# An attention and mixture-of-experts kernel on one core: the vector engines' work of the last part ranked by the step that needs it, and the last two units' steps mixed

## The chip, the cores and the metric

The kernel runs on one core of a Trainium2 chip. The metric is the device time of one execution, in microseconds. The engines go by these names: PE is TensorE's matmuls and PEld its weight loads, DVE is VectorE, ACT is ScalarE, POOL is GpSimd, SP is SyncE, which only issues transfers. Each has its own queue and works through it in the order in which the program was written.

## The reference, cut to what matters

```python
x = attention(q, k, v)                 # 2304 tokens x 512, masks local / strided by head
p = probs / probs.sum(-1)              # 2304 x 4 experts
out = 0
for e in range(4):
    h = relu(x @ w1[e])                # 512 -> 1024
    out += p[:, e:e+1] * (h @ w2[e])   # 1024 -> 512
```

All values are f32, and so is the result.

## The kernel before, in words

The eight pairs of an expert and a half of its hidden channels (512 of 1024) are called units. The tokens are handled in three parts: 384 in a first part that runs beside the attention, 896 in a second (`plan_unit`), and 1024 in the last part (`plan_second`), the only one that the change touches. The last part takes some 300 us of the span.

**The products.** Both layers of a unit are 2x2 block products in Winograd's form of Strassen's scheme: seven products instead of eight. Each product is one step. There are seven h steps for the first layer (P1, s1, s2, s3, s4, P2, a22, named after the block of weights) and seven o steps for the second. A step has two halves f, and each half is six matmuls of 128x128 weights on 512 columns (line 897), since each f32 value is split into a high and a low fp32r part and three of the four partial products are taken. A step is therefore 12 matmuls.

**PSUM.** Steps of kind a (P1, s2, s3, a22) add onto one pair of buffers one after the other; kind b (P2) and kind c (s1, then s4) do so in theirs. The running sum has to be read by another engine after every step, before the next step of the kind adds to it. h steps of kind a use the tag ps (two buffers), o steps of kind a the tag sc (two buffers); kinds b and c use mo (four buffers), except that o P2 uses ps.

**The other engines' work.** After h P2, h s1 and h s4 the product is copied by ACT (line 919, tile v, the code's `park`). After h P1, s2 and s3 DVE adds a parked copy to the product (line 928, `finish`), giving the tile q, and then takes relu and multiplies by the expert's probability, which is laid out along the columns in the tile pb (line 931); after h a22 line 931 alone does this, straight from PSUM. `plan_t` makes the second layer's seven operands T (b11, t1, t2, b22, t3, b21, t4) from q: differences of q blocks (line 960), a high part (ACT, line 955) and a low part (line 956). Lines 956 and 960 can go to DVE or POOL (engine class VP). After each o step DVE adds the product to the tile acc (line 1005). Seven weight blocks per layer and unit are loaded again from DRAM by SP: first layer by `reload` (line 1033), second layer into a ring of four buffers (`plan_ring`, line 983). After the last unit the eight acc tiles are stored (line 1008).

**The order.** PE's order is written out: `TURN` lists 14 steps of a unit, and in it stand the first two h steps of the next unit ("next P2", "next s1") between the h steps of this one:

```python
TURN = ("h P1", "h s4", "h s2", "next P2", "h s3", "next s1", "h a22", "o P1", "o s1", "o s2", "o s4", "o s3", "o P2", "o a22")
```

The last unit has no next unit, so both of those fall away there. The order of the other engines is found by a planner (`Plan.walk`) when the program is built: each operation has a modelled duration and a rank (the last numbers of `add`, written `z`, `zz`), and an engine takes, of the operations that can start earliest, the one of the lowest rank. An operation of class VP goes to the engine that would end it sooner by the model. The planner never lets an engine wait for an operation of better rank. `dz` is the modelled time of half a step (1.365 us). The result is a fixed list for each engine; the chip runs it in that order, with semaphores where an operation needs another's result or buffer.

Before, the rank of an operation was the time of the step that makes its input, with a few half steps added.

Of the kernel before, what the change touches and what calls it, by code (L numbers as in the profile page):

```python
# [11 lines left out]
AF = mybir.ActivationFunctionType  # L12
# [294 lines left out]
def attn_moe_kernel(  # L307
# [13 lines left out]
    nc = tc.nc  # L321
# [587 lines left out]
    def plan_h(u, step, z, dz):  # L909
# [12 lines left out]
        def finish(r, c, nm, f, key, zz):  # L922
            tok = f"q{r}{c}{f}"
            q = lambda: late["q"][r, c, f]
            src = lambda: held[key][:, 0:TH2]
            if nm:
                i = late[nm, f]
                add("DVE", DD, lambda: nc.vector.tensor_tensor(out=q(), in0=src(), in1=late["u"][i], op=ALU.add),  # L928
                    [key, f"u{i}", "late3"], [tok], zz)
            from_q = bool(nm)  # L930
            add("DVE", DD, lambda: nc.vector.scalar_tensor_tensor(  # L931
                out=q(), in0=q() if from_q else src(), scalar=0.0, in1=late["p"][:, c * TH2:c * TH2 + TH2], op0=ALU.max, op1=ALU.mult),
                ["pb", "late3"] + ([] if nm else [key]), [tok], zz + 0.1, two=from_q)

        for f in range(2):
# [5 lines left out]
            if step in PARK:  # L941
                park(f, key, ze)
            else:
                r, c, nm = DONE[step]
                finish(r, c, nm, f, key, ze)

    def plan_t(step, z, dz):
# [4 lines left out]
        def put(v, nm, j, zz):  # L952
            src, tok = v
            hi, lo = (lambda: late["T"][nm][0][j]), (lambda: late["T"][nm][1][j])
            add("ACT", TH2 / 1200 + 0.17, lambda: nc.scalar.activation(out=hi(), in_=src(), func=AF.Copy), [tok, "late3"], [f"T{nm}h{j}"], zz)  # L955
            add("VP", VP, lambda e: engine(e).tensor_tensor(out=lo(), in0=src(), in1=hi().bitcast(F32), op=ALU.subtract),
                [tok, f"T{nm}h{j}"], [f"T{nm}l{j}"], zz)

        def sub(dst, a, b, zz):
            add("VP", VP, lambda e: engine(e).tensor_tensor(out=dst[0](), in0=a[0](), in1=b[0](), op=ALU.subtract), [a[1], b[1]], [dst[1]], zz)  # L960

        for j in range(2):
            if step == "P1":
                put(q[0, 0, j], "b11", j, z)
            elif step == "s2":
                sub(q[0, 0, j], q[0, 1, j], q[0, 0, j], z)
                put(q[0, 0, j], "t1", j, z)
            elif step == "s3":
                sub(q[0, 0, j], q[1, 1, j], q[0, 0, j], z)
                put(q[0, 0, j], "t2", j, z)  # L970
                put(q[1, 1, j], "b22", j, z + 2 * dz)
                sub(q[0, 1, j], q[1, 1, j], q[0, 1, j], z + 4 * dz)
                put(q[0, 1, j], "t3", j, z + 4 * dz)
            else:
                put(q[1, 0, j], "b21", j, z + 2 * dz)
                sub(q[1, 0, j], q[1, 0, j], q[0, 0, j], z + 4 * dz)
                put(q[1, 0, j], "t4", j, z + 4 * dz)
# [9 lines left out]
    acc_count = {}  # L987

    def plan_o(u, step, slot, first, last, z, dz):
# [32 lines left out]
    def plan_second():  # L1022
# [4 lines left out]
        for step in ("P2", "s1"):  # L1027
            plan_h(seq[0], step, zz, dz)
            zz += 2 * dz
# [6 lines left out]
        if NU > 1:  # L1036
            reload("P2", seq[1], zz)
            reload("s1", seq[1], zz)
        for i, u in enumerate(seq):
            v = seq[i + 1] if i + 1 < NU else None  # L1040
            w = seq[i + 2] if i + 2 < NU else None
            slots = {}
            fetch = list(FETCH)
            for _ in range(RING):
                st = fetch.pop(0)
                slots[st] = plan_ring(u, st, zz)
            for what in TURN:
                kind, step = what.split()
                if kind == "next":
                    if v is None:  # L1050
                        continue
                    plan_h(v, step, zz, dz)
                    if w is not None:
                        reload(step, w, zz + 6 * dz)
                elif kind == "h":
                    plan_h(u, step, zz, dz)
                    if step in ("P1", "s2", "s3", "a22"):
                        plan_t(step, zz + 2 * dz, dz)
                    if v is not None:
                        reload(step, v, zz + 6 * dz)  # L1060
                    if step == "a22" and v is not None and units[v][0] != units[u][0]:
                        plan_p(v, zz + 4 * dz)
                else:
                    plan_o(u, step, slots[step], i == 0, i == NU - 1, zz, dz)
                    if fetch:
                        st = fetch.pop(0)
                        slots[st] = plan_ring(u, st, zz)
                zz += 2 * dz
# [225 lines left out]
```

## Time and profile before

| | before |
|---|---|
| device time, median of 3 runs | 824.32 us (823.99 to 825.2) |
| profiled execution, device time | 825.78 us |
| profiled execution, span | 824.0 us |
| PE busy | 810.3 us (98%) |
| DVE busy | 625.2 us (76%) |
| ACT busy | 330.6 us (40%) |
| POOL busy | 308.3 us (37%) |

The span runs from the first to the last instruction; the profiled execution's device time is 1.78 us more. "Busy" is the share of the span in which the engine worked, an average over all parts. PE's busy time counts matmuls, whose ends are modelled.

### The profile page before, as it was taken

How to read it: one execution, taken by the hardware profiler on the slowest of the kernel's cores; microseconds unless marked ns; L12 is line 12 of the kernel's file. 1: busy time of each engine (PE TensorE's matmuls, PEld its weight loads, DVE VectorE, ACT ScalarE, POOL GpSimd, SP SyncE). 2: the span in 40 equal slices, each digit the busy share in tenths (PEclk: the TensorE clock that was granted, in tenths of full speed). 3: DMA queues.
4: the chain of work that ended last, by engine and by line, in shares of the span. 5: the costliest groups of instructions: out<-in, count | busy, mean ns of one | idle time of the engine just before them, and what ended most of it. 6: DMA issues, size and time to landing. Idle time of an engine off the chain costs nothing.

```text
span 824.0 us, 13898 instructions
## 1 busy us (share of the span) xinstructions
PE 810.3 (98%) x5385; PEld 686.0 (83%) x5388; DVE 625.2 (76%) x892; ACT 330.6 (40%) x616; POOL 308.3 (37%) x243
## 2 busy tenths in 40 slices
PE   8999999999999999999999999999999999999987
PEld 6888888999889888888989888887878787878765
DVE  6877867865588776868677693959796979788886
ACT  4643556444336353543535352524142323323140
POOL 5431332934173542515344270305050505142352
PEclk9999999999999999999999999999999999999998
DMA  9685532339578686867753405747474556635714
GB/s 336 218 312 183 204 138 83 102 125 330 211 256 283 258 307 236 324 212 293 260 205 128 175 30 180 278 157 249 148 251 172 188 211 173 232 125 204 208 48 153
DMA packets 70401, 168.69 MB, mean 205 GB/s; under 512 B 5152, under 2 KB 22720, under 8 KB 70336
## 3 DMA queue, kind: packets, MB, share of 16 engines
q1 hardware_dynamic: 70192, 167.73, 57.5%
q8 instruction: 42, 0.69, 0.3%
q14 instruction: 23, 0.19, 0.1%
q10 hardware_dynamic: 144, 0.08, 0.1%
HBM read 108.00 MB, written 59.79 MB: 204 GB/s over the span
## 4 chain that ended last, share of the span: by engine, by line
PE 95%; DVE 1%; DMA 1%; issue 1%; POOL 1%; ACT 0%; POOLq 0%; ACTq 0%
PE mo L897 21%; PE mo L750 17%; PE ps L897 16%; PE sc L897 15%; PE mo L734 8%; PE ps L750 5%; PE sc L750 5%; PE ps L561 2%; PE sc L479 1%; PE ps L533 1%; PE sc L474 1%; DMA qkL<-in_qk_local 1%; PE ps L569 1%; POOL q L960 1%; PE mo L1205 1%
## 5 line engine op out<-in xcount | busy, mean ns | idle before, releaser
L960 POOL TENSOR_TENSOR q<-q,q 128x512 f32<-128x512 f32 x31 | 44.8, 1445 | 211.9 <-DVE q L931 186.2
L750 PE MATMUL mo<-w2t,h 128*128 128x512 f32 x336 | 80.8, 389 | 0.0
L750 PEld LDWEIGHTS mo<-w2t,h 128*128 128x128 f32 x336 | 63.1, 188 | 13.0
L750 PE MATMUL mo<-w2t,hs 128*128 128x512 f32 x288 | 69.9, 395 | 0.0
L750 PEld LDWEIGHTS mo<-w2t,hs 128*128 128x128 f32 x288 | 53.0, 188 | 11.0
L741 DVE SCALAR_TENSOR_TENSOR h<-c,h 128x448 fp32r<-128x448 f32 x48 | 59.6, 1268 | 2.4 <-ACT h L738 1.0
L645 POOL TENSOR_TENSOR a<-raw,a 128x512 fp32r<-128x512 f32 x22 | 34.1, 1549 | 59.6 <-DVE c L1097 44.9
L644 ACT ACTIVATE w2t<-raw 128x512 fp32r<-128x512 f32 x60 | 36.8, 629 | 37.8 <-PE mo L750 24.7
L1005 DVE TENSOR_TENSOR acc<-sc,acc 128x512 f32<-128x512 f32 x58 | 38.7, 684 | 16.4 <-PE sc L897 15.8
L759 DVE SCALAR_TENSOR_TENSOR acc<-mo,pr,acc 128x512 f32<-128x512 f32 x45 | 33.6, 747 | 22.8 <-PE mo L750 22.5
L928 DVE TENSOR_TENSOR q<-ps,v 128x512 f32<-128x512 f32 x48 | 33.1, 689 | 20.6 <-PE ps L897 20.5
L919 ACT ACTIVATE v<-mo 128x512 f32<-128x512 f32 x48 | 28.7, 598 | 49.5 <-PE mo L897 47.9
L645 POOL TENSOR_TENSOR w2t<-raw,w2t 128x512 fp32r<-128x512 f32 x21 | 30.2, 1447 | 46.6 <-ACT w2t L644 44.0
L734 PE MATMUL mo<-xh,a 128*128 128x384 f32 x192 | 46.7, 345 | 0.0
L955 ACT ACTIVATE Tb11h<-q 128x512 fp32r<-128x512 f32 x16 | 10.0, 627 | 84.5 <-DVE q L931 84.5
L644 ACT ACTIVATE wv<-tmp 128x512 fp32r<-128x512 f32 x32 | 20.1, 631 | 58.0 <-POOL tmp L652 12.8
L931 DVE SCALAR_TENSOR_TENSOR q<-q,pb 128x512 f32<-128x512 f32 x48 | 41.1, 857 | 1.1
L750 PE MATMUL ps<-w2t,h 128*128 128x512 f32 x168 | 40.4, 389 | 0.0
L750 PE MATMUL sc<-w2t,h 128*128 128x512 f32 x168 | 40.4, 389 | 0.0
L645 DVE TENSOR_TENSOR w2t<-raw,w2t 128x512 fp32r<-128x512 f32 x39 | 33.9, 897 | 4.5 <-ACT w2t L644 4.5
L750 PEld LDWEIGHTS sc<-w2t,h 128*128 128x128 f32 x168 | 31.5, 188 | 6.5
L750 PEld LDWEIGHTS ps<-w2t,h 128*128 128x128 f32 x168 | 31.5, 188 | 6.5
(261 smaller groups left out, 2108.0 us busy)
## 6 DMA issues: line engine op xcount, KB each, us to landing
raw<-in_w SPq DMA_DIRECT2D x30, 1024.0 KB, 5.9
qkS<-in_qk_strided SPq DMA_DIRECT2D x16, 329.0 KB, 7.9
vstL<-in_v_local SPq DMA_DIRECT2D x8, 640.0 KB, 8.7
out<-acc SPq DMA_DIRECT2D x18, 256.0 KB, 2.0
vstS<-in_v_strided SPq DMA_DIRECT2D x8, 384.0 KB, 8.7
qkL<-in_qk_local SPq DMA_DIRECT2D x8, 336.0 KB, 6.8
pb<-dp SPq DMA_DIRECT2D x5, 512.0 KB, 6.9
qkL<-in_qk_local SPq DMA_DIRECT2D x8, 272.0 KB, 7.6
```

The costliest lines, as they stand in the source:

```text
L644: add("ACT", 0.62, lambda: nc.scalar.activation(out=hi(), in_=src(), func=AF.Copy), need, [name + "h"], z)
L645: add("VP", VP, lambda e: engine(e).tensor_tensor(out=lo(), in0=src(), in1=hi().bitcast(F32), op=ALU.subtract), need + [name + "h"], [name ...
L734: nc.tensor.matmul(pt[:, 0:TA], w[:, c % 2, (f % 2) * P:(f % 2) * P + P], (xl if i == 1 else xh)[c], start=j == 0, stop=j == 11)
L741: nc.vector.scalar_tensor_tensor(out=dst(), in0=src(), scalar=0.0, in1=hi().bitcast(F32), op0=ALU.max, op1=ALU.subtract)
L750: nc.tensor.matmul(pt, ht[f][:, ts], wt[f][:, cs], start=j == 0, stop=j == 11)
L759: nc.vector.scalar_tensor_tensor(out=a, in0=pt, scalar=sc, in1=a, op0=ALU.mult, op1=ALU.add)
L897: nc.tensor.matmul(pt, a[i == 2][:, j, f * P:f * P + P], b[i == 1][j][:, 0:TH], start=bool(first) and n == 0, stop=True, skip_group_check= ...
L919: add("ACT", TH2 / 1200 + 0.18, lambda: nc.scalar.activation(out=late["u"][i], in_=held[key][:, 0:TH2], func=AF.Copy), [key, "late3"], [f" ...
L928: add("DVE", DD, lambda: nc.vector.tensor_tensor(out=q(), in0=src(), in1=late["u"][i], op=ALU.add), [key, f"u{i}", "late3"], [tok], zz)
L931: add("DVE", DD, lambda: nc.vector.scalar_tensor_tensor(out=q(), in0=q() if from_q else src(), scalar=0.0, in1=late["p"][:, c * TH2:c * TH ...
L960: add("VP", VP, lambda e: engine(e).tensor_tensor(out=dst[0](), in0=a[0](), in1=b[0](), op=ALU.subtract), [a[1], b[1]], [dst[1]], zz)
L1005: add("DVE", DD, lambda i=i, key=key: nc.vector.tensor_tensor(out=acc[i], in0=held[key][:, 0:TH2], in1=acc[i], op=ALU.add), [key], tok, zz ...
```

## The change

Operations of the last part get new ranks. A table `due` holds for each unit the planned start of each h and o step. Line 928 is ranked by the next h step that adds to the same buffers, or by the o step that needs its result where that is earlier; line 931 and the T operations by the o step that uses them; the additions of line 1005 by the o step that next uses the same buffers. The list of steps is made for all units at once, and in it three o steps of the last unit but one (s3, P2, a22) stand between h steps of the last unit: s3 before h s3, P2 and a22 before h a22. For these three, kind b uses the tag mo instead of ps. Ring loads are handed out along that list, four o steps ahead, across units. The diff, cut where lines only pass the new argument on:

```diff
...
-        def finish(r, c, nm, f, key, zz):
+        def finish(r, c, nm, f, key, zz, zs):
...
                 add("DVE", DD, lambda: nc.vector.tensor_tensor(out=q(), in0=src(), in1=late["u"][i], op=ALU.add),
-                    [key, f"u{i}", "late3"], [tok], zz)
+                    [key, f"u{i}", "late3"], [tok], min(zz, zs) - 0.8)
             from_q = bool(nm)
             add("DVE", DD, lambda: nc.vector.scalar_tensor_tensor(
                 out=q(), in0=q() if from_q else src(), scalar=0.0, in1=late["p"][:, c * TH2:c * TH2 + TH2], op0=ALU.max, op1=ALU.mult),
-                ["pb", "late3"] + ([] if nm else [key]), [tok], zz + 0.1, two=from_q)
+                ["pb", "late3"] + ([] if nm else [key]), [tok], zs if nm else min(zz, zs), two=from_q)
...
-                finish(r, c, nm, f, key, ze)
...
+                after = {"P1": "s2", "s2": "s3", "s3": "a22"}.get(step)
+                use, ops = {"P1": ("P1", 2), "s2": ("s1", 3), "s3": ("s2", 3), "a22": ("P2", 2)}[step]
+                finish(r, c, nm, f, key, due["h", after] + f * dz if after else ze + 4 * dz, due["o", use] - 1.5 - 0.8 * ops - 0.8 + 0.7 * f)
...
-            add("ACT", TH2 / 1200 + 0.17, lambda: nc.scalar.activation(out=hi(), in_=src(), func=AF.Copy), [tok, "late3"], [f"T{nm}h{j}"], zz)
+            add("ACT", TH2 / 1200 + 0.17, lambda: nc.scalar.activation(out=hi(), in_=src(), func=AF.Copy), [tok, "late3"], [f"T{nm}h{j}"], zz - 1.6)
             add("VP", VP, lambda e: engine(e).tensor_tensor(out=lo(), in0=src(), in1=hi().bitcast(F32), op=ALU.subtract),
-                [tok, f"T{nm}h{j}"], [f"T{nm}l{j}"], zz)
+                [tok, f"T{nm}h{j}"], [f"T{nm}l{j}"], zz - 0.8)
 
         def sub(dst, a, b, zz):
-            add("VP", VP, lambda e: engine(e).tensor_tensor(out=dst[0](), in0=a[0](), in1=b[0](), op=ALU.subtract), [a[1], b[1]], [dst[1]], zz)
+            add("VP", VP, lambda e: engine(e).tensor_tensor(out=dst[0](), in0=a[0](), in1=b[0](), op=ALU.subtract), [a[1], b[1]], [dst[1]], zz - 2.4)
...
+            z = {s: due["o", s] - 1.5 + 0.7 * j for s in STEPS}
             if step == "P1":
-                put(q[0, 0, j], "b11", j, z)
...
             elif step == "s2":
-                sub(q[0, 0, j], q[0, 1, j], q[0, 0, j], z)
-                put(q[0, 0, j], "t1", j, z)
+                sub(q[0, 0, j], q[0, 1, j], q[0, 0, j], z["s1"])
+                put(q[0, 0, j], "t1", j, z["s1"])
             elif step == "s3":
-                sub(q[0, 0, j], q[1, 1, j], q[0, 0, j], z)
-                put(q[0, 0, j], "t2", j, z)
-                put(q[1, 1, j], "b22", j, z + 2 * dz)
-                sub(q[0, 1, j], q[1, 1, j], q[0, 1, j], z + 4 * dz)
-                put(q[0, 1, j], "t3", j, z + 4 * dz)
+                sub(q[0, 0, j], q[1, 1, j], q[0, 0, j], z["s2"])
+                put(q[0, 0, j], "t2", j, z["s2"])
+                put(q[1, 1, j], "b22", j, z["s4"])
+                sub(q[0, 1, j], q[1, 1, j], q[0, 1, j], z["s3"])
+                put(q[0, 1, j], "t3", j, z["s3"])
             else:
-                put(q[1, 0, j], "b21", j, z + 2 * dz)
-                sub(q[1, 0, j], q[1, 0, j], q[0, 0, j], z + 4 * dz)
-                put(q[1, 0, j], "t4", j, z + 4 * dz)
+                put(q[1, 0, j], "b21", j, z["P2"])
+                sub(q[1, 0, j], q[1, 0, j], q[0, 0, j], z["a22"])
+                put(q[1, 0, j], "t4", j, z["a22"])
...
+    tags = {"a": "sc", "b": "ps", "c": "mo"}
+
+    def plan_o(u, step, slot, first, last, z, dz, due):
...
-            key = ({"a": "sc", "b": "ps", "c": "mo"}[kk], "o" + kk, u, f)
+            key = (tags[kk], "o" + kk, u, f)
             zz = z + f * dz
+            after = {"P1": "s2", "s2": "s3", "s3": "a22", "s1": "s4"}.get(step)
+            zd = (due["o", after] + f * dz if after else zz + 5 * dz) - 0.8
...
-                add("AD", ad(TH2), lambda e, i=i, key=key: copy(e, lambda: acc[i], key, lambda pt: pt[:, 0:TH2]), [key], tok, zz + dz)
+                add("AD", ad(TH2), lambda e, i=i, key=key: copy(e, lambda: acc[i], key, lambda pt: pt[:, 0:TH2]), [key], tok, zd)
             else:
                 add("DVE", DD, lambda i=i, key=key: nc.vector.tensor_tensor(
-                    out=acc[i], in0=held[key][:, 0:TH2], in1=acc[i], op=ALU.add), [key], tok, zz + dz)
+                    out=acc[i], in0=held[key][:, 0:TH2], in1=acc[i], op=ALU.add), [key], tok, zd)
...
         plan_p(seq[0], zz)
-        for step in ("P2", "s1"):
-            plan_h(seq[0], step, zz, dz)
-            zz += 2 * dz
 
...
-        if NU > 1:
-            reload("P2", seq[1], zz)
-            reload("s1", seq[1], zz)
-        for i, u in enumerate(seq):
-            v = seq[i + 1] if i + 1 < NU else None
-            w = seq[i + 2] if i + 2 < NU else None
...
+        tasks = [("next", -1, "P2"), ("next", -1, "s1")]
+        for i in range(NU):
             for what in TURN:
                 kind, step = what.split()
-                if kind == "next":
-                    if v is None:
-                        continue
-                    plan_h(v, step, zz, dz)
-                    if w is not None:
-                        reload(step, w, zz + 6 * dz)
-                elif kind == "h":
-                    plan_h(u, step, zz, dz)
-                    if step in ("P1", "s2", "s3", "a22"):
-                        plan_t(step, zz + 2 * dz, dz)
-                    if v is not None:
-                        reload(step, v, zz + 6 * dz)
-                    if step == "a22" and v is not None and units[v][0] != units[u][0]:
-                        plan_p(v, zz + 4 * dz)
-                else:
-                    plan_o(u, step, slots[step], i == 0, i == NU - 1, zz, dz)
-                    if fetch:
-                        st = fetch.pop(0)
-                        slots[st] = plan_ring(u, st, zz)
-                zz += 2 * dz
+                tasks.append((kind, i, step))
+        tasks = [t for t in tasks if t[0] != "next" or t[1] + 1 < NU]
+        late_o = [("o", NU - 2, step) for step in ("s3", "P2", "a22")]
+        tasks = [t for t in tasks if t not in late_o]
+        for t, before in zip(late_o, (("h", NU - 1, "s3"), ("h", NU - 1, "a22"), ("h", NU - 1, "a22"))):
+            tasks.insert(tasks.index(before), t)
+        os = [t for t in tasks if t[0] == "o"]
+        due = [{} for _ in range(NU)]
+        for n, (kind, i, step) in enumerate(tasks):
+            due[i + (kind == "next")][kind[0] if kind != "next" else "h", step] = zz + 2 * dz * n
+        slots = {t: plan_ring(seq[t[1]], t[2], zz) for t in os[:RING]}
+        for t in tasks:
+            kind, i, step = t
+            if kind == "o":
+                tags["b"] = "mo" if t in late_o else "ps"
+                plan_o(seq[i], step, slots[t], i == 0, i == NU - 1, zz, dz, due[i])
+                n = os.index(t) + RING
+                if n < len(os):
+                    slots[os[n]] = plan_ring(seq[os[n][1]], os[n][2], zz)
+            else:
+                i += kind == "next"
+                plan_h(seq[i], step, zz, dz, due[i])
+                if step in ("P1", "s2", "s3", "a22"):
+                    plan_t(step, due[i])
+                if i + 1 < NU:
+                    reload(step, seq[i + 1], zz + 6 * dz)
+                    if step == "a22" and units[seq[i + 1]][0] != units[seq[i]][0]:
+                        plan_p(seq[i + 1], zz + 4 * dz)
+            zz += 2 * dz
...
```

## Rows read from the trace of the kernel before

**Rows 1.** The page: busy time by engine, PE and granted clock in 40 slices.

```profile
PE 810.3 (98%) x5385; PEld 686.0 (83%) x5388; DVE 625.2 (76%) x892; ACT 330.6 (40%) x616; POOL 308.3 (37%) x243
...
PE   8999999999999999999999999999999999999987
...
PEclk9999999999999999999999999999999999999998
```

**Rows 2.** Windows by unit, and the end: busy us of each engine, granted clock, DMA.

```profile
core 0: us, PE busy (x) PEld busy (x) DVE busy (x) ACT busy (x) POOL busy (x), PEclk, DMA share, GB/s
728.16:767.23 39.07, 38.83 (x168) 31.37 (x169) 32.64 (x43) 11.85 (x21) 11.99 (x9) 1.00 0.46 162
767.23:800.00 32.77, 31.24 (x134) 24.87 (x135) 26.94 (x36) 7.40 (x13) 9.46 (x7) 1.00 0.40 113
800.00:810.00 10.00, 7.82 (x28) 6.05 (x27) 7.58 (x10) 3.36 (x7) 8.63 (x6) 0.83 0.31 105
```

**Rows 3.** Waits of PEld after 500 us: total, times, longest, all in us.

```profile
PEld sc L897 <- issue: 6.3, 7, 2.6
PEld mo L897 <- DVE acc L1005: 2.5, 6, 0.4
PEld ps L897 <- DVE q L928: 2.3, 2, 2.0
PEld ps L897 <- DMA ring<-d26a: 0.2, 1, 0.2
```

**Rows 4.** Timeline of PE in a middle unit: start, us, then the instructions.

```profile
764.12 0.61 PE L897 MATMUL mo<-Tt1h,ring 128*128 128x512 f32 x2
...
767.23 0.70 PE L897 MATMUL sc<-Tt2h,ring 128*128 128x512 f32 x2 [0.24 <-issue]
...
770.06 0.62 PE L897 MATMUL mo<-Tb22h,ring 128*128 128x512 f32 x2
...
773.08 0.62 PE L897 MATMUL sc<-Tt3h,ring 128*128 128x512 f32 x2
...
775.80 0.62 PE L897 MATMUL ps<-Tb21h,ring 128*128 128x512 f32 x2
```

**Rows 5.** Timeline of DVE in the same unit.

```profile
763.55 0.68 DVE L956 TENSOR_TENSOR Tb22l<-q,Tb22h 128x512 fp32r<-128x512 f32 x1
...
764.76 1.18 DVE L956 TENSOR_TENSOR Tt2l<-q,Tt2h 128x512 fp32r<-128x512 f32 x1
...
766.46 1.27 DVE L1005 TENSOR_TENSOR acc<-sc,acc 128x512 f32<-128x512 f32 x2
767.65 1.36 DVE L956 TENSOR_TENSOR Tb21l<-q,Tb21h 128x512 fp32r<-128x512 f32 x1
...
769.53 1.40 DVE L956 TENSOR_TENSOR Tt4l<-q,Tt4h 128x512 fp32r<-128x512 f32 x1
770.85 0.68 DVE L1005 TENSOR_TENSOR acc<-mo,acc 128x512 f32<-128x512 f32 x1
771.46 0.68 DVE L956 TENSOR_TENSOR Tt4l<-q,Tt4h 128x512 fp32r<-128x512 f32 x1
```

**Rows 6.** The chain that ended last, through the last unit.

```profile
781.40 2.77 PE ps L897 x12
...
797.60 3.47 POOL q L960 x2
...
804.79 4.56 PE sc L897 x12
...
817.51 2.73 PE sc L897 x12
...
820.27 0.69 DVE acc L1005
```

**Rows 7.** Groups by line after 500 us: count, busy us, mean ns, idle before.

```profile
L960 POOL TENSOR_TENSOR q<-q,q 128x512 f32<-128x512 f32 x31 | 44.8, 1445 | 211.9 <-DVE q L931 186.2 <-ACT Tt1h L955 21.4 <-DVE Tb21l L956 3.8
...
L1005 DVE TENSOR_TENSOR acc<-sc,acc 128x512 f32<-128x512 f32 x58 | 38.7, 684 | 16.4 <-PE sc L897 15.8
L960 DVE TENSOR_TENSOR q<-q,q 128x512 f32<-128x512 f32 x33 | 36.4, 1103 | 0.3
L928 DVE TENSOR_TENSOR q<-ps,v 128x512 f32<-128x512 f32 x48 | 33.1, 689 | 20.6 <-PE ps L897 20.5
```

More of the change, by code (lines that the diff above doesn't have):

```diff
@@ L907, in attn_moe_kernel, with plan_h @@
     rcnt = [0]
-    def plan_h(u, step, z, dz):
+    def plan_h(u, step, z, dz, due):
         a, b, kk, first_in = STEPS[step]
@@ L944, in plan_h, with plan_t @@
                 r, c, nm = DONE[step]
-                finish(r, c, nm, f, key, ze)
-    def plan_t(step, z, dz):
+                after = {"P1": "s2", "s2": "s3", "s3": "a22"}.get(step)
+                use, ops = {"P1": ("P1", 2), "s2": ("s1", 3), "s3": ("s2", 3), "a22": ("P2", 2)}[step]
+                finish(r, c, nm, f, key, due["h", after] + f * dz if after else ze + 4 * dz, due["o", use] - 1.5 - 0.8 * ops - 0.8 + 0.7 * f)
+    def plan_t(step, due):
         q = {(r, c, j): (lambda r=r, c=c, j=j: late["q"][r, c, j], f"q{r}{c}{j}") for r in range(2) for c in range(2) for j in range(2)}
@@ L959, in sub @@
         def sub(dst, a, b, zz):
-            add("VP", VP, lambda e: engine(e).tensor_tensor(out=dst[0](), in0=a[0](), in1=b[0](), op=ALU.subtract), [a[1], b[1]], [dst[1]], zz)
+            add("VP", VP, lambda e: engine(e).tensor_tensor(out=dst[0](), in0=a[0](), in1=b[0](), op=ALU.subtract), [a[1], b[1]], [dst[1]], zz - 2.4)
         for j in range(2):
+            z = {s: due["o", s] - 1.5 + 0.7 * j for s in STEPS}
             if step == "P1":
-                put(q[0, 0, j], "b11", j, z)
+                put(q[0, 0, j], "b11", j, z["P1"])
@@ L987, in attn_moe_kernel @@
     acc_count = {}
-    def plan_o(u, step, slot, first, last, z, dz):
+    tags = {"a": "sc", "b": "ps", "c": "mo"}
+    def plan_o(u, step, slot, first, last, z, dz, due):
         a, b, kk, first_in = STEPS[step]
@@ L1034, in reload @@
                 z, xfer=((1.45, 128),))
-        if NU > 1:
-            reload("P2", seq[1], zz)
-            reload("s1", seq[1], zz)
-        for i, u in enumerate(seq):
-            v = seq[i + 1] if i + 1 < NU else None
-            w = seq[i + 2] if i + 2 < NU else None
-            slots = {}
-            fetch = list(FETCH)
-            for _ in range(RING):
-                st = fetch.pop(0)
-                slots[st] = plan_ring(u, st, zz)
+        tasks = [("next", -1, "P2"), ("next", -1, "s1")]
@@ L1047, in plan_second @@
+        for i in range(NU):
             for what in TURN:
                 kind, step = what.split()
-                if kind == "next":
-                    if v is None:
-                        continue
-                    plan_h(v, step, zz, dz)
-                    if w is not None:
-                        reload(step, w, zz + 6 * dz)
-                elif kind == "h":
-                    plan_h(u, step, zz, dz)
-                    if step in ("P1", "s2", "s3", "a22"):
-                        plan_t(step, zz + 2 * dz, dz)
-                    if v is not None:
-                        reload(step, v, zz + 6 * dz)
-                    if step == "a22" and v is not None and units[v][0] != units[u][0]:
-                        plan_p(v, zz + 4 * dz)
-                else:
-                    plan_o(u, step, slots[step], i == 0, i == NU - 1, zz, dz)
-                    if fetch:
-                        st = fetch.pop(0)
-                        slots[st] = plan_ring(u, st, zz)
```

## Prediction, made before the result was known

> **What bounds the kernel now.** The page comes first: TensorE is busy 810.3 of 824.0 us and its granted clock is full in all slices but one or two at the end [rows 1]. No matmul is removed, so only TensorE's waits can be won, and the question is which waits of the last part the change can reach.
>
> The windows by unit come next. A middle unit is 39.07 us long and VectorE works 32.64 us of it, so over the whole unit VectorE has 6.4 us to spare [rows 2]. The list of waits of TensorE's weight loads names few: seven before the sc products on Tt2h (no releaser named, longest 2.6 us), six of some 0.4 us on the addition of line 1005, and two on line 928, nearly all of it in one of 2.0 us [rows 3]. Six of the seven and all six of the second kind come once in each of the six middle units; the rest is in the last unit.
>
> The timeline of TensorE in a middle unit gives their size. The starts of o s1, s2, s4, s3 and P2 lie 3.11, 2.83, 3.02 and 2.72 us apart [rows 4]. Twelve undisturbed matmuls take 2.72 us, so the excess is 0.39 + 0.11 + 0.30 = 0.80 us per unit.
>
> VectorE's timeline says why [rows 5]. The product o s2 goes into the same two sc buffers as o P1, so it can't start before line 1005 has read P1's first half. P1's first half was through by some 763 us (half of its 2.72 us before s1 starts at 764.12 [rows 4]), but the addition ran at 766.46, behind Tb22l (763.55) and Tt2l (764.76) among others. TensorE started s2 at 767.23, some 0.1 us after that addition's first half was done. In the same way o s4 adds onto s1's mo buffers: s1's second half is read at 770.85, behind Tb21l (767.65) and Tt4l (769.53), neither of which is needed before 775 us. This is a wrong order on VectorE, not missing time.
>
> The last unit has no next unit to put between its steps. The chain runs through it from 781.40 to 820.24 us, 38.84 us for 12 steps [rows 6]; at 2.72 us each they would be 32.64 us. The excess is 6.20 us: 2.0 us waiting for line 928, ahead of a22's second half [rows 3]; 1.84 us because s2's twelve matmuls took 4.56 us instead of 2.72; and the rest, some 2.4 us, ahead of s2, where the weight loads waited 2.6 us [rows 3]. s2 ran at a granted clock that had fallen after the gap: it is 0.83 on average from 800 to 810 us and 1.00 in the windows before [rows 2] (between the levels of 2.4 and 1.2 GHz).
>
> **The change part by part.** It adds and removes no instruction of TensorE, VectorE, ScalarE or GpSimd in the last part. It gives most other engines' operations there a rank from the step that needs them, and moves three o steps (3 x 12 matmuls, and their six additions of line 1005) of the last unit but one into the last unit.
>
> *New ranks, middle units.* In the planner's microseconds from a unit's start (a step is 2.73), the old ranks were: Tt2l 13.7, Tb22l 16.4, line 931 for a22 17.8, Tt3l 19.1, P1's addition 20.5, Tb21l 21.8, s1's additions 23.2 and 24.6, Tt4l 24.6. That is the order seen in [rows 5]. The new ones are: Tt2l 22.3 and 23.0, line 931 for a22 23.2 and 24.6, P1's additions 23.8 and 25.1, Tb22l 25.0 and 25.7, s1's additions 26.5 and 27.9, Tt3l 27.7, Tb21l 30.5, Tt4l 33.2. Tb22l falls behind P1's first addition, and Tb21l and Tt4l behind both of s1's. One operation of VectorE less ahead of P1's first half (0.6 us at the least) is more than the 0.39 us missing there; two less ahead of s1's second half (Tb21l 1.36 us, Tt4l 1.40 us [rows 5]) are more than the 0.30 us.
>
> What is late next? Tb21l and Tt4l now come after additions of 0.69 us. They ended at 769.01 and 772.14 us [rows 5] and are wanted at 775.80 [rows 4] and, a step later, at 778.52, so four additions in front of them (2.8 us) still leave Tb21l 4.0 us and Tt4l 3.6 us. Line 928, which frees the ps buffers for the next h step, gets ranks below those of the T operations. So: the gain is at most 6 x 0.80 = 4.8 us, at least nothing (the order of the engines could leave the additions where they are); I take 6 x 0.70 = 4.2, near the upper bound, because the missing 0.3 to 0.4 us is smaller than any one operation that steps back.
>
> *Three o steps mixed into the last unit.* The order becomes h P1, s4, s2, old s3, h s3, old P2, old a22, h a22, and then the seven o steps. Nothing is added to TensorE: the same 36 matmuls stand elsewhere. Between h s2 and h a22 there are now 4 x 2.72 us of other work instead of one step. The wait for line 928 (2.0 us) is covered by old P2 and old a22 (5.4 us), and s2 is reached 8.2 us later after h P1 than now, while the T work ahead of it was 2.4 us late. VectorE gets six additions (6 x 0.69 = 4.1 us) into these 8.2 us, so about 4 us are won net, against waits of 2.0 and 2.4 us that follow one from the other. Without the gap there is no fall of the clock. The gain is at most 6.2 us, at least nothing; I take 5.6 (the chain of q, T and line 1005 is long, and a few tenths may stay).
>
> *What is moved besides.* Old P2's products go to the mo tag instead of ps, because h takes ps; mo has four buffers, and those that it takes over were last read by ScalarE's line 919, three steps earlier as I count the rotation: nothing, hidden by those steps; if the copy is late it costs up to one step of 2.72 us. Old a22's additions must be read before o P1 takes the sc buffers again; h a22 (2.72 us) stands between and covers 2 x 0.69. The ring loads of SP's queue are planned across units, but still held back to 14 us before their use; the only wait of TensorE for one is 0.2 us long [rows 3], so I count nothing, with 0.2 us either way per unit as bounds. Reloads of line 1033 keep their steps. Out stores and the tail behind the last matmul (820.24 to 824.0) stay.
>
> *Sum.* 4.2 + 5.6 = 9.8 us; bounds 0 and 11.0. The profiled execution took 825.78 us, 1.78 more than its span, so it would take 816.0; the median of the runs shown is 824.32, 1.46 below it, and the same saving gives **814.5 us**.
>
> **The shared bandwidth of VectorE and GpSimd** is the place where the new order could fail. Line 960, two SBUF tensors, takes 1103 ns on VectorE on average, while lines 928 and 1005, which read one input from PSUM, take 689 and 684 [rows 7]: the first is stretched when GpSimd works, the others not. (The Trainium skill, GPSIMD Engine Reference, Specifications, states the same: GpSimd contends with VectorE's instructions that have two SBUF inputs. By it, additions of line 1005 beside GpSimd's work are free, and two-SBUF work is not.) If the planner now gives GpSimd more, each such operation (1445 ns [rows 7]) costs VectorE some 0.4 to 1.1 us.
>
> **Rivals.**
> 1. *The middle units keep their gaps* and only the last unit is mended. For it: the same gap in six units in a row could be a shortage of sc buffers. (The Trainium skill, Perfetto Trace Analysis, Identifying Performance Opportunities, Optimization Strategy, reads consistent bubbles so; in this trace it would leave the 0.39 us where it is.) Against it: P1's half lay finished for some 3 us while VectorE did other things [rows 5]. Time: 824.3 - 5.6 = 818.7.
> 2. *The last unit keeps a part of its waits*, since six additions and line 928 press on VectorE together. Against it: the 4 us net. If half of 6.2 stays: 824.3 - 4.2 - 3.1 = 817.0.
> 3. *Slower*: the t4 chain (line 960, Tt4h, Tt4l), now ranked last, is late for o a22 in every unit. It is 3.6 us early by the count above; with several more operations on GpSimd that is used up. From 9.8 / 8 = 1.2 us of wait per unit on the change loses; at 2 us per unit the time is 824.3 - 9.8 + 16 = 830.5.
> 4. *No effect*: the planner, which takes whatever is ready first, gives nearly the same order, and the last unit's waits move to its o steps: 824.
>
> **How the numbers follow.** Forecast 0.75, rival 1 0.09, rival 2 0.06, rival 3 0.06, rival 4 0.04. Within the forecast the time lies between 813.0 (all of 11.0 won, 0.3 for the runs) and 816.5 (7.8 won). The range reaches over rivals 1 and 2: 812.8 to 819.0. A measurement of this kernel tells about 0.2% (1.6 us) from no change. Faster: the forecast and rivals 1 and 2, less a little for mixtures, 0.89; same 0.04; slower 0.07.
>
> **What would show it.** Right: the weight loads' waits on line 1005 gone and no gap before Tt2h in the middle units, units of 38.2 to 38.4 us; full clock to the end; the last matmul done near 810.4 us (820.24 - 9.8), the tail of 3.8 us as before. Wrong: waits before Tb21h or Tt4h; waits of h steps on lines 928 or 919; a ring load awaited; GpSimd clearly busier than 308 us and VectorE's line 960 well above 1103 ns.

## The result, and the profile after

The changed kernel takes 813.34 us (median of 4 runs, 812.86 to 813.72) against 824.76 us (823.99 to 826.58) in the same comparison: a ratio of 0.9858, with a 95% interval of 0.984 to 0.9876. Its profiled execution took 813.42 us, with a span of 811.6 us. The forecast was 814.5 us.

The page of the changed kernel, to be read against [rows 1]:

```profile
PE 803.5 (99%) x5385; PEld 684.8 (84%) x5388; DVE 608.0 (75%) x860; ACT 328.2 (40%) x615; POOL 354.7 (44%) x276
...
PE   8999999999999999999999999999999999999998
...
PEclk9999999999999999999999999999999999999999
```

PE's busy time is 6.8 us shorter with the same matmuls, and the clock row is full to the end. The windows by unit (to [rows 2]): a middle unit, the last unit but one up to the first of the mixed steps, and everything from there to the last matmul.

```profile
core 0: us, PE busy (x) PEld busy (x) DVE busy (x) ACT busy (x) POOL busy (x), PEclk, DMA share, GB/s
698.33:736.56 38.23, 38.23 (x169) 31.54 (x168) 30.21 (x38) 11.51 (x20) 17.56 (x12) 1.00 0.55 193
736.56:766.63 30.07, 30.07 (x133) 24.79 (x132) 25.26 (x31) 11.51 (x20) 17.56 (x12) 1.00 0.67 219
766.63:807.85 41.22, 41.22 (x181) 33.61 (x179) 32.41 (x44) 9.69 (x16) 19.95 (x14) 1.00 0.39 133
```

PE is busy for the whole of each window. A middle unit takes 38.23 us instead of 39.07. The waits of the weight loads after 500 us, which filled [rows 3], are now one line:

```profile
PEld sc L897 <- issue: 0.2, 1, 0.2
```

VectorE's timeline of a middle unit, beside [rows 5] (lines 1005, 960 and 956 are now 1011, 962 and 958):

```profile
714.20 1.78 DVE L958 TENSOR_TENSOR Tb22l<-q,Tb22h 128x512 fp32r<-128x512 f32 x1
...
717.61 1.28 DVE L931 SCALAR_TENSOR_TENSOR q<-ps,pb 128x512 f32<-128x512 f32 x2
718.81 0.68 DVE L958 TENSOR_TENSOR Tt2l<-q,Tt2h 128x512 fp32r<-128x512 f32 x1
719.41 0.68 DVE L1011 TENSOR_TENSOR acc<-sc,acc 128x512 f32<-128x512 f32 x1
720.44 0.69 DVE L1011 TENSOR_TENSOR acc<-sc,acc 128x512 f32<-128x512 f32 x1 [0.35 <-PE sc L897]
721.05 1.40 DVE L958 TENSOR_TENSOR Tb21l<-q,Tb21h 128x512 fp32r<-128x512 f32 x1
722.37 1.48 DVE L1011 TENSOR_TENSOR acc<-mo,acc 128x512 f32<-128x512 f32 x2
...
726.57 1.28 DVE L1011 TENSOR_TENSOR acc<-sc,acc 128x512 f32<-128x512 f32 x2
727.77 0.92 DVE L958 TENSOR_TENSOR Tt4l<-q,Tt4h 128x512 fp32r<-128x512 f32 x1
```

P1 begins at 717.51 us, its first half is through some 1.4 us later, and the addition runs at 719.41, with Tt2l and line 931 just in front of it: 1.90 us after P1's start, where it was 5.08 us before (766.46 after 761.38). Both of s1's (722.37) run ahead of Tt4l (727.77). One half of Tb21l still stands before them, but in time. GpSimd does twelve operations in the unit, where it did eight, among them a half of Tt2l that VectorE did before:

```profile
715.39 1.75 POOL L958 TENSOR_TENSOR Tt2l<-q,Tt2h 128x512 fp32r<-128x512 f32 x1
717.11 1.74 POOL L958 TENSOR_TENSOR Tb22l<-q,Tb22h 128x512 fp32r<-128x512 f32 x1
```

The chain that ended last, beside [rows 6], is nothing but PE steps of 2.72 to 2.77 us until the last addition, s2 (794.26) right behind s1:

```profile
766.80 2.77 PE ps L897 x12
...
791.54 2.72 PE mo L897 x12
794.26 2.72 PE sc L897 x12
...
805.14 2.73 PE sc L897 x12
...
807.89 0.69 DVE acc L1011
```

**Where the time went.** The spans differ by 12.4 us, but 1.5 us of that lies ahead of the changed part: the first h step of the last part starts at 503.18 us before and at 501.66 us after, and the instructions ahead of it are the same. In the twelve further kernels, which don't touch that part either, it starts at 501.1 to 504.1 us. So the length of the last part, from its first h matmul to its last o matmul, is the better measure. It is 317.05 us before and 306.19 us after: 10.86 us less. Up to the first step that is mixed (773.08 us before, 766.63 us after) the change won 4.93 us, and from there on 5.93 us.

### The profile page after: what moved, and what is told of

The parts are those of the page before. It is cut to its first block, busy times and chain, and to the rows that moved or that the text cites. A ratio compares the mean times of both kernels' runs of the same rounds, so it can differ in the third digit from the quotient of the medians.

```text
span 811.6 us, 13933 instructions
## 1 busy us (share of the span) xinstructions
PE 803.5 (99%) x5385; PEld 684.8 (84%) x5388; DVE 608.0 (75%) x860; ACT 328.2 (40%) x615; POOL 354.7 (44%) x276
## 4 chain that ended last, share of the span: by engine, by line
PE 97%; DVE 1%; ACT 0%; issue 0%; POOL 0%; ACTq 0%
PE mo L897 22%; PE mo L750 18%; PE ps L897 17%; PE sc L897 15%; PE mo L734 8%; PE ps L750 5%; PE sc L750 5%; PE ps L561 2%; PE sc L479 1%; PE ps L533 1%; PE ps L569 1%; PE sc L474 1%; PE mo L1208 1%; DVE wv L645 0%; DVE pmS L496 0%
## 5 line engine op out<-in xcount | busy, mean ns | idle before, releaser
L962 POOL TENSOR_TENSOR q<-q,q 128x512 f32<-128x512 f32 x41 | 60.9, 1492 | 143.5 <-DVE q L931 142.6
L741 DVE SCALAR_TENSOR_TENSOR h<-c,h 128x448 fp32r<-128x448 f32 x48 | 61.3, 1305 | 2.4 <-ACT h L738 1.0
L962 DVE TENSOR_TENSOR q<-q,q 128x512 f32<-128x512 f32 x23 | 32.7, 1420 | 6.4 <-POOL Tb21l L958 6.2
```

What stands on the lines that cost most here:

```text
L741: nc.vector.scalar_tensor_tensor(out=dst(), in0=src(), scalar=0.0, in1=hi().bitcast(F32), op0=ALU.max, op1=ALU.subtract)
```

## The experiments

For each kernel the table gives the device time (median), the ratio to the kernel before as it was measured alongside (823.9 to 824.8 us) with its 95% interval, the length of the last part and that of a middle unit (from one o P1 to the next), both from PE's timeline.

| kernel | us | ratio (interval) | last part, us | middle unit, us |
|---|---|---|---|---|
| before | 824.76 | | 317.05 | 39.04 |
| the change | 813.34 | 0.9858 (0.984 to 0.9876) | 306.19 | 38.23 |
| ranks only | 818.04 | 0.9928 (0.9909 to 0.9948) | 311.78 | 38.23 |
| mixed steps only | 824.0 | 0.9998 (0.9986 to 1.001) | 316.18 | 39.03 |
| additions first | 816.2 | 0.9909 (0.9889 to 0.9929) | 308.11 | 38.23 |
| additions' new rank alone | 828.66 | 1.0062 (1.0039 to 1.0085) | 322.12 | 39.04 |
| change, no GpSimd | 814.14 | 0.9879 (0.9862 to 0.9896) | 306.16 | 38.23 |
| change, one step mixed | 813.04 | 0.9862 (0.9848 to 0.9877) | 306.09 | 38.23 |
| three mixed, additions first | 814.54 | 0.9877 (0.986 to 0.9893) | 306.16 | 38.23 |
| change, additions' old rank | 813.15 | 0.9864 (0.985 to 0.9879) | 306.38 | 38.23 |
| one mixed, additions first | 814.87 | 0.9882 (0.9866 to 0.9899) | 307.27 | 38.23 |
| ranks only, no GpSimd | 814.64 | 0.9882 (0.9868 to 0.9897) | 306.85 | 38.23 |
| before, no GpSimd | 819.57 | 0.9937 (0.9922 to 0.9951) | 311.90 | 38.25 |
| additions first, no GpSimd | 815.78 | 0.9892 (0.9875 to 0.9908) | 308.30 | 38.23 |

### The two halves of the change, each alone

Ranks only: the list of moved steps is empty.

```diff
-        late_o = [("o", NU - 2, step) for step in ("s3", "P2", "a22")]
+        late_o = []
```

> The new ranks, without the three steps mixed into the last unit. My theory (two causes, each with its own cure): the middle units lose their gaps (38.2 us each instead of 39.07), some 4.9 us; the last unit keeps most of its 6 us, since nothing stands between h s3 and h a22. 817.5 to 820.5 us against some 824.8 before. Rival (the last unit's waits too are only a wrong order): at most 815 us, and the last unit within 1 us of 12 x 2.72.

The middle units came to 38.23 us and the total to 818.04 us, as my theory had it; the last unit kept 5.6 us (311.78 less 306.19). Its waits of the weight loads:

```profile
PEld sc L897 <- ACT Tb21h L957: 3.3, 1, 3.3
PEld ps L897 <- DVE q L928: 1.2, 2, 0.7
```

The first line names Tb21h, which is no operand of s2. The weight loads began at 797.59 us, right behind the end of P1's addition (796.84 and 0.68 us), and VectorE's timeline ahead of it gives the chain. The columns are start and duration:

```profile
789.47 3.48 DVE L962 TENSOR_TENSOR q<-q,q 128x512 f32<-128x512 f32 x2
792.87 3.45 DVE L958 TENSOR_TENSOR Tt2l<-q,Tt2h 128x512 fp32r<-128x512 f32 x2
...
796.84 0.68 DVE L1011 TENSOR_TENSOR acc<-sc,acc 128x512 f32<-128x512 f32 x1
```

The two differences of t2 and their two low parts take 6.9 us for four operations, two and a half times as long as four undisturbed ones (0.69 us each), and P1's addition comes after them. What stretches them is tried below.

Mixed steps only: the change's list of steps, with `plan_h`, `plan_t` and `plan_o` ranking as before.

```diff
-                plan_h(seq[i], step, zz, dz, due[i])
+                plan_h(seq[i], step, zz, dz)
-                    plan_t(step, due[i])
+                    plan_t(step, zz + 2 * dz, dz)
```

> The three steps mixed into the last unit, with the old ranks. My theory: the last unit is cured (some 5.9 us less) and the six middle units keep 39.07 us, with the weight loads still waiting for the addition of the product to acc: 818 to 820 us. Rival (the old ranks also spoil the mixed unit, because the added additions fall behind the T work): the last unit keeps 2 us or more of its waits, 821 us or more.

Here my theory failed and the rival held: 824.0 us, nothing won that can be measured. The middle units' waits on the addition stayed, and the long wait ahead of an sc product grew from 2.6 to 3.8 us:

```profile
PEld sc L897 <- issue: 7.5, 7, 3.8
PEld mo L897 <- DVE acc L1006: 2.7, 6, 0.5
```

It stands in another place now, ahead of o P1:

```profile
796.89 1.08 PE L897 MATMUL sc<-Tb11h,ring 128*128 128x512 f32 x2 [3.39 <-issue]
```

VectorE's timeline says why:

```profile
793.21 1.27 DVE L1006 TENSOR_TENSOR acc<-mo,acc 128x512 f32<-128x512 f32 x2
794.41 1.78 DVE L956 TENSOR_TENSOR Tt2l<-q,Tt2h 128x512 fp32r<-128x512 f32 x1
796.11 1.28 DVE L1006 TENSOR_TENSOR acc<-sc,acc 128x512 f32<-128x512 f32 x2
```

Old a22's additions to acc (796.11) come behind the T work, and o P1 can't take the sc buffers before them. So the wait that the mixed steps cover ahead of s2 comes back two steps earlier, ahead of o P1. Mixed steps by themselves add additions to the very queue that is in the wrong order.

### Which of the ranks count

Additions first: the kernel before, with one number changed.

```diff
-                    out=acc[i], in0=held[key][:, 0:TH2], in1=acc[i], op=ALU.add), [key], tok, zz + dz)
+                    out=acc[i], in0=held[key][:, 0:TH2], in1=acc[i], op=ALU.add), [key], tok, zz + dz - 8)
```

> The kernel before with one number changed: the additions of the o products to acc get a rank 8 us earlier, so that they come first on VectorE. My theory (only VectorE's order makes the gaps of the middle units): middle units of 38.2 to 38.4 us, 4.0 to 4.9 us less in all, 819.5 to 821 us; the last unit keeps at least 4 of its 6 us. Rival (a shortage of PSUM buffers makes the gaps): no change, 824 to 826 us. Second rival (the rest of the ranks is needed, since the T work then comes late): the gaps move to the T operands, less than 2 us won or a loss.

The middle units lost their gaps, with the same PSUM buffers: the gaps were no shortage of buffers. It won more than expected, 8.9 us of the last part's 10.9, because in the last unit too the wait ahead of s2 and the slow matmuls behind it were gone. One wait is left, the one on line 928 ahead of h a22's second half:

```profile
PEld ps L897 <- DVE q L928: 2.3, 2, 2.0
```

Additions' new rank alone: the kernel before, with only the change's rank of the additions.

```diff
+            zd = (zz + 4 * dz if step in ("P1", "s2", "s3", "s1") else zz + 5 * dz) - 0.8
-                    out=acc[i], in0=held[key][:, 0:TH2], in1=acc[i], op=ALU.add), [key], tok, zz + dz)
+                    out=acc[i], in0=held[key][:, 0:TH2], in1=acc[i], op=ALU.add), [key], tok, zd)
```

> The kernel before with the change's ranks for the additions alone (they are later than the old ones by 3 us or more), everything else ranked as before. My theory (what counts is the additions' place among the T work, not their rank as such): P1's addition also falls behind Tb21l and s1's behind both halves of Tt4l, so each middle unit loses 0.6 to 2 us more: 828 to 837 us. Rival (the additions' ranks by the step that needs the buffer carry the gain): 819 to 821 us.

The sign and the total were as expected (828.66 us), the place was not: the middle units stayed at 39.0 us (one took 39.4), and of 5.1 us lost in the last part 3.6 are in the last unit, most of the rest in the first (a ring load). In the last unit P1's addition was put behind Tt3l and Tb21l as well, and s2 begins 8.40 us after s1 instead of 5.07:

```profile
801.99 1.81 DVE L956 TENSOR_TENSOR Tt2l<-q,Tt2h 128x512 fp32r<-128x512 f32 x1 [1.18 <-ACT Tt2h L955]
803.72 1.74 DVE L956 TENSOR_TENSOR Tt3l<-q,Tt3h 128x512 fp32r<-128x512 f32 x1
805.39 1.74 DVE L956 TENSOR_TENSOR Tb21l<-q,Tb21h 128x512 fp32r<-128x512 f32 x1
807.05 0.68 DVE L1006 TENSOR_TENSOR acc<-sc,acc 128x512 f32<-128x512 f32 x1
```

So a rank is only worth what it does among the operations that are ready at the same time. In the middle units the T operations that now had the better rank were not ready yet.

The change with the additions' old rank (the end of their own product), the rest by need:

```diff
-            zd = (due["o", after] + f * dz if after else zz + 5 * dz) - 0.8
+            zd = zz + dz
```

> The changed kernel with the additions' old rank (the end of their own product), which is earlier than their new one by some 3 us or more. Theory A (what counts is that the additions stand ahead of the T work that is not urgent; late ranks for the T work are enough for that): as the changed kernel, 812.5 to 814.5 us. Rival (the additions need the rank of the step that waits for their buffer): middle gaps or a wait of h s2, h s3 on line 928 come back, 815 us or more.

813.15 us, as the change. The additions need no rank by need; they need only stand ahead of T work that is not urgent, and late ranks for the T work do that.

### How many steps must be mixed

One step only:

```diff
-        late_o = [("o", NU - 2, step) for step in ("s3", "P2", "a22")]
+        late_o = [("o", NU - 2, step) for step in ("a22",)]
```

> The changed kernel with one o step (a22 of the last unit but one) mixed into the last unit instead of three. Theory A (each mixed step covers 2.7 us of the last unit's chain from h s3 to o s2, where ranks alone left some 5.7 us of waits and slow clock): 2 to 3.5 us of the 4.7 us between ranks only and the whole change are won, 814.5 to 816.3 us. Rival (the wait is short of a threshold, and once TensorE does not idle before s2 the clock holds too): all of it, 813 to 814 us. Second rival (the wait on line 928 ahead of h a22 alone is covered): 816.5 to 818 us.

The first rival held: 813.04 us and a last part of 306.09 us. One step of 2.7 us covers all that ranks alone had left, slow clock included. My theory, a gain in proportion to the steps, is wrong.

Three mixed steps and the additions first, all other ranks as before:

```diff
-                    out=acc[i], in0=held[key][:, 0:TH2], in1=acc[i], op=ALU.add), [key], tok, zz + dz)
+                    out=acc[i], in0=held[key][:, 0:TH2], in1=acc[i], op=ALU.add), [key], tok, zz + dz - 8)
```

> The three steps mixed and the additions to acc ranked 8 us earlier, all other ranks as before the change. Theory A (of the new ranks only the place of the additions ahead of the T work matters): no waits in the middle units and the last, 812.5 to 814.5 us, as the whole change. Rival (the T operations' ranks by need are wanted as well, for the mixed unit): 815 us or more, with waits of the last unit for T operands.

The last part is as short as with the whole change (306.16 us) and has no wait. The time is 814.54 us, just above the 814.5 that was expected at most; 4.9 us of its span lie behind the last matmul instead of 3.8, as in the run with the additions first, and the cause of that is open.

One mixed step and the additions first (both edits shown above):

> The kernel before with the additions to acc ranked 8 us earlier and only the o step a22 of the last unit but one mixed into the last unit; no rank by need for anything else. Theory (these two edits are all of the change that counts): no waits of TensorE in the last part, whose length is 306.0 to 306.5 us as with the whole change, 812.5 to 814.5 us. Rival (with one mixed step only, the T operations' new ranks are needed to get the last unit's T work done in time): the wait on line 928 or a T operand comes back, 815 us or more.

It missed its mark narrowly, 814.87 us: the last part is 1.1 us too long, with a wait of 0.8 us on line 928 ahead of h a22 and one of 0.6 us on a ring load in the first unit. With the old ranks one step is not quite enough.

### What stretches VectorE

The change, with the T operations on VectorE alone:

```diff
-            add("VP", VP, lambda e: engine(e).tensor_tensor(out=lo(), ...
+            add("DVE", VP[0], lambda e="DVE": engine(e).tensor_tensor(out=lo(), ...
```

(and the same for line 962)

> The changed kernel with the T operations of the last part on VectorE alone, so that GpSimd rests there. Theory A (VectorE has room: 50 operations of 0.65 us are 32.5 us of a unit's 38.2, and each operation on GpSimd stretches VectorE's two-SBUF operations anyway): middle units stay at 38.2 us, 812.5 to 814.5 us, as the changed kernel. Rival (GpSimd's share is what keeps VectorE's queue short between h s3 and o s3): TensorE waits again in every unit, 816 us or more.

The last part is 306.16 us, the same as with GpSimd; the time of 814.14 us lies within the scatter of the start (its profiled span has 504.08 us ahead of the last part). The groups of VectorE's operations after 500 us, first of the change, then of this kernel (mean ns behind the busy time):

```profile
L1011 DVE TENSOR_TENSOR acc<-sc,acc 128x512 f32<-128x512 f32 x58 | 39.1, 685 | 17.1 <-PE sc L897 16.7
L928 DVE TENSOR_TENSOR q<-ps,v 128x512 f32<-128x512 f32 x48 | 33.1, 690 | 25.5 <-PE ps L897 25.4
L962 DVE TENSOR_TENSOR q<-q,q 128x512 f32<-128x512 f32 x23 | 32.7, 1420 | 6.4 <-POOL Tb21l L958 6.2
```

```profile
L962 DVE TENSOR_TENSOR q<-q,q 128x512 f32<-128x512 f32 x64 | 42.0, 686 | 0.0
L1011 DVE TENSOR_TENSOR acc<-sc,acc 128x512 f32<-128x512 f32 x58 | 39.9, 689 | 12.6 <-PE sc L897 12.1
L928 DVE TENSOR_TENSOR q<-ps,v 128x512 f32<-128x512 f32 x48 | 33.2, 692 | 23.4 <-PE ps L897 23.0
```

Line 962, with two SBUF inputs, takes 686 ns each without GpSimd and 1420 ns with it. Lines 928 and 1011, with one input from PSUM, take the same in both. The windows of one middle unit, first of the kernel before, then of this one (VectorE and GpSimd are the third and fifth pair):

```profile
703.13:742.20 39.07, 38.83 (x169) 31.39 (x168) 32.65 (x42) 11.88 (x20) 12.00 (x8) 1.00 0.54 189
```

```profile
698.30:736.60 38.30, 38.30 (x170) 31.61 (x169) 31.94 (x51) 11.82 (x20) 0.00 (x0) 1.00 0.55 192
```

With eight operations of a unit on GpSimd VectorE is busy 32.65 us, and with none on GpSimd 31.94 us. The kernel before itself, without GpSimd, comes to 31.71 us (its window stands below). So handing GpSimd eight of the operations had made VectorE's own work longer. In the change, with other ranks, GpSimd gets twelve, and VectorE is busy 30.21 us: 1.7 us less than without it, for twelve operations that alone would take VectorE 8.2 us (0.69 us each).

Ranks only, without GpSimd (the two edits shown above):

> The new ranks without the mixed steps, and the T operations of the last part on VectorE alone. Theory (in the last unit VectorE is stretched by GpSimd's work on SBUF: between 783.7 and 796.3 us of the run with ranks only, eight of its operations took 11.7 us instead of some 5, while GpSimd did eight operations that would be 5 us on VectorE): the wait ahead of s2 gets shorter by 1 to 3 us, 815 to 817.5 us against 818.0. Rival (GpSimd carries a real share of the last unit's work): 819 us or more. Second rival (the chain of single operations decides, not VectorE's load): 817.5 to 818.5 us.

It won more than expected: 814.64 us, and a last part of 306.85 us instead of 311.78. What is left against the change, 0.7 us, lies at o s4, which waits for additions to be done with the mo buffers. The same operations as in the run with ranks only, here without GpSimd beside them:

```profile
788.99 1.29 DVE L962 TENSOR_TENSOR q<-q,q 128x512 f32<-128x512 f32 x2
...
790.79 1.29 DVE L958 TENSOR_TENSOR Tt2l<-q,Tt2h 128x512 fp32r<-128x512 f32 x2
791.99 0.69 DVE L1011 TENSOR_TENSOR acc<-sc,acc 128x512 f32<-128x512 f32 x1
```

The four operations of t2 take 2.6 us instead of 6.9, and P1's addition runs 4.6 us earlier, counted from the unit's start (774.21 and 774.48 us). So all but 0.7 us of what the mixed steps cover, given the ranks, is time that GpSimd's work on SBUF takes from VectorE.

The kernel before, without GpSimd:

> The kernel before (old ranks, no mixed steps) with the T operations of the last part on VectorE alone. Theory A (the additions' place in VectorE's queue is a cause of its own): the weight loads still wait for the addition in the middle units, 39.0 us or more each, while the last unit loses 2 us or more of its 6; 819 to 822.5 us. Rival (GpSimd's stretching of VectorE's two-SBUF operations is what makes the additions late): middle units of at most 38.5 us, 817 us or less.

The total (819.57 us) fell into theory A's range, but its reason did not hold: the middle units are 38.25 us, by the rival's words. VectorE's timeline of a middle unit and its window:

```profile
758.04 1.28 DVE L956 TENSOR_TENSOR Tt3l<-q,Tt3h 128x512 fp32r<-128x512 f32 x2
759.24 0.68 DVE L1005 TENSOR_TENSOR acc<-sc,acc 128x512 f32<-128x512 f32 x1
```

```profile
716.99:755.25 38.26, 38.26 (x170) 31.50 (x169) 31.71 (x51) 11.64 (x20) 0.00 (x0) 1.00 0.49 167
```

The addition comes behind both halves of Tt3l, as it is ranked, but the queue in front of it is so much shorter that it is in time: it runs 3.99 us after o P1's start (755.25) instead of 5.08. In the last unit the order does cost:

```profile
PEld sc L897 <- DVE acc L1005: 2.3, 1, 2.3
PEld ps L897 <- DVE q L928: 2.2, 2, 1.7
```

The additions first, without GpSimd:

> The kernel before with the additions ranked 8 us earlier and the T operations on VectorE alone; no ranks by need, no mixed steps. Theory B (after the run with ranks only and without GpSimd: once VectorE is not stretched and the additions stand in front, nothing else is needed): last part of 306 to 307.5 us, 813 to 815 us. Rival (without ranks by need the last unit's wait on line 928 ahead of h a22 stays, as the 2.0 us with the additions first alone): 815.5 to 817 us.

The rival held: 815.78 us, with the wait on line 928 of 2.2 us left, as with GpSimd.

```profile
PEld ps L897 <- DVE q L928: 2.2, 2, 1.7
PEld sc L897 <- DVE Tt3l L956: 0.4, 1, 0.4
```

The two cures of the middle units don't add up; either is enough. The wait on line 928 goes with late ranks for the T work (ranks only had 1.2 us of it left, in two waits) or with mixed steps.

No kernel beat the change by more than the measurement can tell: the best, with one step mixed, lies 0.04% below it.

## Why the prediction came out right, and which of its steps did not hold

**The bound.** TensorE's waits in the last part were all there was to win, and the change won all of them: one wait of 0.2 us is left. The total of 10.86 us lies between the value taken (9.8) and the upper bound (11.0).

**New ranks, middle units.** Taken at 4.2 us, at most 4.8; measured 4.93 us up to the first mixed step. The term was mis-sized by keeping back a part of each gap: all of it went, and 0.1 us of the first unit besides. That the additions stood in a wrong order is shown by the one changed number, which gave 38.23 us per unit. But "a wrong order on VectorE, not missing time" is only half of it: without GpSimd the old order gives 38.25 us too. The order was too late because GpSimd's work had stretched the queue. And the addition did not come forward in the way that the prediction told. Tb22l was to fall behind it by rank, but in every middle unit of the change both halves of Tb22l run ahead of it (714.20 on VectorE, 717.11 on GpSimd in the unit shown): they ran before P1's first half was through, and a rank counts only among operations that are ready. What went from in front of the addition is a difference (line 960, now 962) and a half of Tt2l, which GpSimd took over. The prediction had named a larger share of GpSimd as a danger only. So the first gap of each unit, 0.39 of the 0.80 us, closed in another way than the one told, and that its size came out is in part luck; that an earlier place of the addition closes it is shown by the run with the additions first, not by the change. Of the operations in front of s1's additions Tt4l fell behind as told, Tb21l in one half of two.

**Mixed steps.** Taken at 5.6 us, at most 6.2; measured 5.93 us from there on. Of these the ranks alone give 0.34 (ranks only: 5.59 us longer than the change), so the mixed steps on top of the ranks give 5.59, which is the value taken. In its working the 1.84 us for the slow matmuls are 0.16 too many, since the chain's 4.56 us reach to the last matmul's end and 2.72 goes from start to start; from start to start s2 took 4.40 us (804.79 to 809.19). The step that failed is that this gain stood beside the ranks as a term of its own. Alone the mixed steps win nothing (0.9998), because the additions that they bring stand among the T work, and those of old a22 hold up o P1. The prediction's sentence that about 4 us are won net counted VectorE's time and not its order. Its rival 2 named the mechanism, additions and line 928 pressing on VectorE together, but gave it half of the excess, where without the ranks it took all. And one mixed step does what I had counted three for.

**Rival 1** (the middle units keep their gaps) fell. The Trainium skill, Perfetto Trace Analysis, Identifying Performance Opportunities, Optimization Strategy, says that consistent bubbles can mean a shortage of SBUF or PSUM; here the same gap came back in six units and went with the buffers unchanged.

**Rival 3** (t4 late) fell: in the unit shown Tt4l ended by 728.7 us, and o a22, six steps after o P1's start at 717.51, needed it at 733.9.

**Rival 4** (no effect, the last unit's waits move to its o steps, 824) fell for the whole change. It is what the mixed steps do without the ranks: 824.0 us, with the wait at o P1.

**The sign for GpSimd misled.** I had named a busier GpSimd and a line 960 well above 1103 ns as signs of failure. Both came (354.7 us of GpSimd instead of 308.3, and 1420 ns), and the time was still won: in the last part TensorE's weight loads waited 0.2 us in all, so no stretched operation came too late for a step.

## What to carry to other kernels

When the bounding engine waits a few tenths of a microsecond at the same place of every round, look at what stands in the releaser's own queue ahead of the operation that frees the buffer: an addition that frees PSUM belongs ahead of work for later steps, and a rank changes only the order among operations ready at the same time and, through the planner, which engine takes them. Filling a thin last round with steps of the one before pays only once that order is right, since the steps bring their own additions along. And before sharing two-input work on SBUF between VectorE and GpSimd, time the kernel with and without it. VectorE's busy time doesn't settle it: with ranks only it is 30.21 us per middle unit with GpSimd and 31.86 without, and yet the last part is 4.9 us longer with it.

## What the runs showed of the hardware that I had not expected

GpSimd's help won no time here: without it the last part is as long to 0.2 us in the change (306.16 us) and with the additions first (308.30), and some 5 us shorter in the kernel before and with ranks only. A 128x512 f32 operation with two SBUF inputs takes 0.69 us on VectorE alone and up to 1.79 us beside GpSimd's, while the same on GpSimd takes 1.29 us alone and up to 1.8 us beside VectorE's: where both work on such operations without a break, the two engines together do two of them in some 1.75 us, and VectorE alone would do two and a half. The Trainium skill, GPSIMD Engine Reference, Specifications, says that the SBUF interfaces are shared and contended with VectorE's instructions of two SBUF inputs; the runs agree, and show that the price can be more than the help (eight operations per unit, 32.65 us of VectorE against 31.71) or most of it (twelve, 30.21 against 31.94).

TensorE waited 2.2, 2.9, 3.4 and 5.5 us ahead of an o step in the kernel before, with ranks only, with mixed steps only and with the additions' new rank alone. Each time the 12 matmuls of that step took 4.4 to 4.6 us from start to start instead of 2.72, at a granted clock of 0.58 to 0.61 over the step (an average of the two levels, 2.4 and 1.2 GHz). In the kernel before without GpSimd a wait of 1.9 us lay between the two halves of s2, and the next step took 4.0 us at 0.66. Behind the waits of 1.5 us inside h a22 there was nothing of the kind. So the 2.2 us wait of the last unit cost nearly twice its length.
